# Attention plus gated FFN on one core: head groups in pairs, OUT in two parts, prologue evictions to the idler engine, and a new order of work

## The chip, the core and the metric

The kernel runs on one core of one Trainium2 chip. The metric is the time of one execution in device microseconds (us). A core has several engines that run side by side (in the kernel before, PE, ACT and DVE are busy 90%, 89% and 86% of the same span): PE (matrix multiply, with its own weight loads, PEld), ACT (ScalarE), DVE (VectorE), POOL (GpSimd) and SP (here only a queue that issues DMAs). A run that is over 1.5% above the fastest of its kernel would be called slow. "Clock" is the share of the full PE clock that was granted in the records; it is a mean over a stretch.

## The reference, cut to what matters

```python
xn = layernorm(x)                                   # 2048 rows x 512, no scale, no bias
q, k, v = split_heads(xn @ wqkv)                    # 32 heads of 16
o = softmax(q @ k.T / 4) @ v                        # full attention, 2048 x 2048 per head
out = x + o @ wo + (silu(xn @ w1) * (xn @ w3)) @ w2 # F = 1792
```

The exponentials of attention are most of the work: 32 heads of 2048 x 2048 scores.

## The kernel before: the parts that matter

The rows of queries are cut into 4 chunks of 512 and the heads into 8 groups of 4. One (chunk, group) is a *unit*; there are 32. A unit has 64 score tiles of 128 x 512, which are made and used in *pairs* of two tiles, so there are 1024 pairs in all. A pair's exponentials are taken either by ACT (one instruction) or by DVE (a bit trick in five instructions). PV then multiplies them with V, and an extra column of ones gives the row sums. At the end of a unit a chain copies PV's result to U, moves the sums, inverts them, spreads the inverses over the rows (DMAs to Lc, Rrow, R) and multiplies: the result is a tile of `onorm`.

What is neither scores nor PV is called *dense* work here: Q, K and V tiles, FFN steps (14 per chunk, 8 groups of 4 matmuls each) and OUT tiles (4 per chunk; each sums FFN rows and attention rows into 128 rows of the result).

The order of instructions on each engine is fixed while the kernel is built. A planner in the Python code simulates the engines with modelled durations and emits instructions in the order in which its model would start them. Where a model was wrong, an engine waits in that order: in the changed kernel's trace PE stands 2.06 us before 644 us, for one late multiply, with scores behind it.

```python
# what PE takes next, in this order
elif try_a() or try_d() or try_pv() or try_dense():      # ACT scores, DVE scores, PV, dense

# FFN of a chunk waits for all of OUT of the chunk before
if sc > 0 and not all(("OUT", (sc - 1) * 4 + i) in done for i in range(4)):
    return False

# OUT: 14 groups over FFN rows, then 8 over attention rows (4 heads x 16 rows of 128 used)
for fc in range(FC):
    gr.append((hT[:, fc, ...], w2[:, fc, :], ...))
for g in range(NG):                                      # NG = 8
    gr.append((onorm[:, (qc * NG + g) % NON, ...], wo[:, g, :], ...))

# prologue: one score buffer, no DVE exponentials while "early"
bufs = [0]
if not st["early"] and idle((2, 3)):
    bufs = [0, 1]
# ... (cut)
```

## Time and profile before

| | value | where it is read |
|---|---|---|
| time | 887.0 us, median of 4 runs (883.5 to 888.4) | timed runs |
| busy over the span | PE 90%, ACT 89%, DVE 86% | page, part 1 |
| last exponential on ACT starts at | 825.3 us | instructions of the exp line |
| last FFN eviction starts at | 857.6 us | instructions of its line |

Three lines of the page of the kernel before: the busy time of each engine over the whole span, then for ACT the busy tenths and for PE the granted clock in tenths, in 40 slices of 22.2 us.

```profile
PE 797.7 (90%) x8985; PEld 223.4 (25%) x8985; DVE 766.3 (86%) x999; ACT 791.6 (89%) x885; POOL 59.4 (7%) x59
ACT  2689999999889999999999999999999999999310
PEclk9999999999569999999999999999999999999878
```

The averages alone mislead: three engines near 90% look balanced. The strips show stages. Counted from 1, ACT is full from slice 4 to slice 37 apart from a dent at slices 11 and 12, just where the clock falls to 5 and 6 tenths, and it is all but idle in the last three.

The same by stretches, from the windows view of the kernel before. Columns: stretch and its length, busy us and number of instructions of PE, PEld, DVE, ACT and POOL, then granted clock, DMA share and GB/s.

```profile
54.00:220.00 166.00, 152.59 (x1695) 41.20 (x1693) 154.51 (x196) 164.94 (x187) 7.69 (x6) 0.99 0.27 38
220.00:260.00 40.00, 38.39 (x246) 7.00 (x244) 30.67 (x36) 34.87 (x36) 2.58 (x2) 0.53 0.19 15
260.00:640.00 380.00, 354.59 (x3998) 95.76 (x3996) 350.69 (x440) 376.31 (x419) 23.61 (x15) 1.00 0.25 32
640.00:660.00 20.00, 17.99 (x194) 4.79 (x190) 19.51 (x25) 19.46 (x23) 1.56 (x1) 1.00 0.29 35
660.00:827.00 167.00, 156.56 (x1802) 42.86 (x1804) 156.24 (x200) 165.51 (x184) 9.42 (x7) 1.00 0.26 33
827.00:886.00 59.00, 38.03 (x559) 15.51 (x553) 16.13 (x29) 3.59 (x6) 0.00 (x0) 0.79 0.20 39
```

In the long stretches ACT is busy 99% of the time: the exponentials set the pace, and dense work gets what PE has over. In 220:260 ("the hole") PE is 96% busy and yet runs only 246 matmuls, at a clock of 0.53: FFN of chunk 0 is done, FFN of chunk 1 must wait for OUT, and OUT for the last unit's chain. This is why PE's busy share can't be read as PE's progress: at that clock (0.50 in 222:258) a score matmul shows 0.60 us, at full clock (270:400) 0.39.

In 827:886 ("the tail") ACT has nothing to do. Three lines of the timeline of the kernel before show why; the bracket at the end of a line is the idle time before it and what ended it.

```profile
829.72 1.32 PE L1222 MATMUL ps<-f_xnT,f_w 128*32 128x512 bf16 x12 [2.32 <-DMA f_w<-in_B_w_dram]
835.82 2.74 PE L1222 MATMUL ps<-f_xnT,f_w 128*32 128x512 bf16 x32 [2.83 <-DMA f_w<-in_B_w_dram]
842.20 3.60 PE L1222 MATMUL ps<-f_xnT,f_w 128*32 128x512 bf16 x32 [3.64 <-DMA f_w<-in_B_w_dram]
```

Seven FFN steps are left over after attention, PE waits four times for their weights from HBM (2.3 to 3.6 us each), and all of the last chunk's OUT comes after them.

### The profile page before, as it was taken

To read this page: it belongs to the slowest core of one execution; us is meant where nothing else is said; L and a number is where in the kernel's file an instruction comes from. 1 tells how busy PE (TensorE), PEld (TensorE's weight loads), DVE (VectorE), ACT (ScalarE), POOL (GpSimd) and SP (SyncE) were. 2 spreads that over 40 slices of the span, in tenths; PEclk is the share of its full clock that TensorE was granted. 3 is DMA by queue.
4 is the path that set the end of the run, shared out by engine and by line. 5 is a ranking of instruction groups with operands and counts; after the bars stand their busy time and mean duration, and the time that the engine had idled before them with its cause. 6 is when DMAs were issued, how large, how long until landed. Compare 5 with 4: busy or idle time off the path is not lost.

```text
span 886.3 us, 21031 instructions
## 1 busy us (share of the span) xinstructions
PE 797.7 (90%) x8985; PEld 223.4 (25%) x8985; DVE 766.3 (86%) x999; ACT 791.6 (89%) x885; POOL 59.4 (7%) x59
## 2 busy tenths in 40 slices
PE   4899998998999999999989999989889999989586
PEld 1322222222112222222222222222222222222132
DVE  6879998999778999989989999989999999999332
ACT  2689999999889999999999999999999999999310
POOL 4200001000000000011000000000000000000000
PEclk9999999999569999999999999999999999999878
DMA  8713223123112223221322223231222222333311
GB/s 306 170 31 50 31 38 55 26 37 38 7 14 26 21 27 45 28 43 29 48 32 20 32 26 38 38 37 26 33 30 44 20 26 20 44 44 38 50 26 40
DMA packets 88471, 38.42 MB, mean 43 GB/s; under 512 B 71472, under 2 KB 85552, under 8 KB 88368
## 3 DMA queue, kind: packets, MB, share of 16 engines
q1 hardware_dynamic: 88368, 36.99, 27.4%
q8 instruction: 72, 1.18, 0.6%
q14 instruction: 31, 0.25, 0.1%
HBM read 22.81 MB, written 2.10 MB: 28 GB/s over the span
## 4 chain that ended last, share of the span: by engine, by line
ACT 60%; PE 20%; DVE 15%; DMA 2%; issue 2%; SPq 0%; DVEq 0%
ACT f_PT L1571 57%; PE ps L1222 10%; PE ps L1533 6%; DVE f_xd L1623 5%; PE ps L1736 4%; DVE f_xd L1669 3%; ACT f_th L1350 2%; DVE f_xd L1683 2%; DVE f_xd L1662 1%; DVE f_xd L1678 1%; DMA f_w<-in_B_w_dram 1%; DMA f_wkv<-in_A_wqkv_dram 1%; DVE f_hT L1364 1%; DVE f_t L1354 1%; DVE f_xn_sb L1412 1%
## 5 line engine op out<-in xcount | busy, mean ns | idle before, releaser
L1571 ACT ACTIVATE f_PT<-ps 128x1024 bf16<-128x1024 f32 x810 | 761.3, 1094 | 21.4 <-PE ps L1533 18.1
L1533 PE MATMUL ps<-f_QT,f_KT 32*128 32x512 bf16 x2048 | 330.2, 395 | 38.7 <-ACT f_PT L1571 30.1
L1623 DVE TENSOR_SCALAR f_xd<-ps 128x1024 int16<-128x1024 f32 x214 | 261.2, 1221 | 33.9 <-PE ps L1533 26.4
L1736 PE MATMUL ps<-f_PT,f_Vaug 128*17 128x512 bf16 x1620 | 232.3, 394 | 5.1 <-DVE f_xd L1678 1.6
L1736 PE MATMUL ps<-f_xd,f_Vaug 128*17 128x512 bf16 x1284 | 182.0, 393 | 3.0 <-DVE f_xd L1683 0.9
L1222 PE MATMUL ps<-f_xnT,f_w 128*32 128x512 bf16 x1792 | 157.2, 401 | 18.2 <-DMA f_w<-in_B_w_dram 11.4
L1533 PEld LDWEIGHTS ps<-f_QT,f_KT 32*128 32x128 bf16 x2048 | 82.0, 91 | 355.6 <-ACT f_PT L1571 312.6
L1669 DVE TENSOR_TENSOR f_xd<-f_xd 128x2048 bf16<-128x2048 bf16 (+1 forms) x119 | 132.4, 1112 | 0.0
L1789 POOL TENSOR_TENSOR f_onorm<-f_U,f_R 128x512 bf16<-128x512 f32 x31 | 44.9, 1447 | 733.6 <-DMA f_R<-f_Rrow 529.8
L1662 DVE TENSOR_SCALAR f_xd<-f_xd 128x2048 int16<-128x2048 int16 (+1 forms) x119 | 78.8, 662 | 6.3 <-PE ps L1736 4.1
L1683 DVE TENSOR_SCALAR f_xd<-f_xd 128x2048 int16<-128x2048 int16 (+1 forms) x119 | 82.0, 689 | 2.0
L1678 DVE TENSOR_SCALAR f_xd<-f_xd 128x2048 int16<-128x2048 int16 (+1 forms) x119 | 78.3, 658 | 2.6
L1736 PEld LDWEIGHTS ps<-f_PT,f_Vaug 128*17 128x17 bf16 x1620 | 53.4, 88 | 104.7 <-issue 85.1
L1222 PE MATMUL ps<-f_w,f_hT 128*32 128x512 bf16 x896 | 71.9, 386 | 1.7 <-DVE f_hT L1364 1.3
L1350 ACT ACTIVATE f_th<-ps 128x512 f32<-128x512 f32 x56 | 38.0, 679 | 26.9 <-PE ps L1222 26.9
L1222 PEld LDWEIGHTS ps<-f_xnT,f_w 128*32 128x32 bf16 x1792 | 42.0, 98 | 75.0 <-issue 48.2
L1736 PEld LDWEIGHTS ps<-f_xd,f_Vaug 128*17 128x17 bf16 x1284 | 41.1, 88 | 43.9 <-issue 22.3
L1354 DVE SCALAR_TENSOR_TENSOR f_t<-f_th,ps 128x512 bf16<-128x512 f32 x56 | 38.2, 683 | 13.4 <-ACT f_th L1350 13.1
L1364 DVE SCALAR_TENSOR_TENSOR f_hT<-f_t,ps 128x512 bf16<-128x512 bf16 x56 | 38.2, 682 | 13.1 <-PE ps L1222 12.9
L1222 PE MATMUL ps<-f_wo,f_onorm 128*32 128x512 bf16 x512 | 40.2, 381 | 0.2 <-DVE f_wkv L1404 0.2
L1222 PEld LDWEIGHTS ps<-f_w,f_hT 128*32 128x32 bf16 x896 | 20.8, 96 | 23.0 <-issue 9.5
L1222 PE MATMUL ps<-f_wkv,f_xnT 128*32 128x512 bf16 x256 | 21.3, 434 | 3.5 <-DMA f_wkv<-in_A_wqkv_dram 3.5
(52 smaller groups left out, 220.4 us busy)
## 6 DMA issues: line engine op xcount, KB each, us to landing
f_w<-in_B_w_dram SPq DMA_DIRECT2D x112, 128.0 KB, 3.0
f_R<-f_Rrow SPq DMA_DIRECT2D x128, 32.0 KB, 4.4
f_KT<-f_hT SPq DMA_DIRECT2D x6, 512.0 KB
f_KT<-f_stg SPq DMA_DIRECT2D x32, 64.0 KB, 1.9
f_QT<-f_stg SPq DMA_DIRECT2D x32, 64.0 KB, 3.1
f_xr<-in_A_x_dram SPq DMA_DIRECT2D x16, 128.0 KB, 2.2
out_dram<-f_xn_sb SPq DMA_DIRECT2D x16, 128.0 KB
f_w<-in_B_w_dram SPq DMA_DIRECT2D x1, 1792.0 KB
```

The lines of the kernel that those rows point to most:

```text
L1222: ins = e.matmul(bank(bk)[32 * i:32 * i + 32, 0:ncols], make_lhsT(i), rhs_ap, start=start, stop=stop, tile_position=(0, 32 * i))
L1350: q = P.op("act", lambda e: e.activation(th[:, ss, :], bank(bk), ACTF.Tanh, scale=0.5), reads=[("ps", bk)], writes=[("th", ss)], dur=a_cos ...
L1354: q2 = P.op("dve", lambda e: e.scalar_tensor_tensor(t1[:, ss, :], th[:, ss, :], 1.0, bank(bk), ALU.add, ALU.mult), reads=[("th", ss), ("ps ...
L1364: q = P.op("dve", lambda e: e.scalar_tensor_tensor(hT[:, fc, :], t1[:, ss, :], 0.5, bank(bk), ALU.mult, ALU.mult), reads=[("t1", ss), ("ps ...
L1533: ins = e.matmul(bank(b), l_, r_, start=True, stop=True, tile_position=(rp, 0))
L1571: q = P.op("act", lambda e: e.activation(PT[:, s_, :], ps[:, b0 * 512:(b0 + 2) * 512], ACTF.Exp, scale=ASC, bias=ABIAS), reads=[("ps", b0) ...
L1623: q = P.op("dve", lambda e: e.tensor_scalar(dsl[:, ys, 1024 * c:1024 * c + 1024], ps[:, 4 * 512:6 * 512], 0.0, 32767.0, ALU.max, ALU.min), ...
L1662: P.op("dve", lambda e: e.tensor_scalar(dsl[:, NY + m_, 0:n], y, 0x7F, 0x3F00, ALU.bitwise_and, ALU.bitwise_or), reads=[("ds", ys)], write ...
L1669: q_ = P.op("dve", lambda e: e.tensor_tensor(t_ap.bitcast(BF16), y.bitcast(BF16), t_ap.bitcast(BF16), ALU.mult), reads=[("ds", ys)], write ...
L1678: q_ = P.op("dve", lambda e: e.tensor_scalar(g_ap, y, -352.0, 0.0, ALU.add, ALU.max), reads=[("ds", ys)], writes=[("ds", NY + NM + g_)] + ...
L1683: q_ = P.op("dve", lambda e: e.tensor_scalar(y, y, 0x7F80, None, ALU.bitwise_and), reads=[], writes=[("ds", ys)], dur=s_cost(n), name="e")
L1736: ins = e.matmul(bank(PV)[32 * j:32 * j + 17, :], v_, p_, start=s0, stop=s1, tile_position=(0, 32 * j))
```

## The change

Its intent, part by part:

- **Group pairs** (of head groups; not the pairs of score tiles above). Two head groups share one tile of `onorm` and one of `wo`: the odd unit's result sits in rows 16 to 31 of each 32. OUT has 4 attention groups in place of 8 (64 groups of 4 matmuls fewer in all). PV of odd units has 32 weight columns in place of 17 to land in those rows, and 64 small DMAs move the rows together.
- **Split.** OUT of chunks 0 to 2 becomes an FFN part (added to x, kept in `osum`) and an attention part. FFN of the next chunk waits only for the FFN part.
- **Prologue.** An eviction of V or of a transpose goes to whichever of ACT and DVE is idle first; two score buffers; no FFN before the early tiles are done; DVE exponentials from the last transpose on.
- **Order.** PE takes dense work before PV while fewer than `PVQ` = 8 PV tasks wait.

```diff
-    NON = 11
+    NON = 6
+    NP = NG // 2
+    PVQ = 8
...
-        wo = sb("wo", [128, NG, D], BF16)
+        wo = sb("wo", [128, NP, D], BF16)
...
-                P.post("dve", emit, ready=o.end + _LAT, prio=prio)
+                P.post2({"dve": emit, "act": emit_a}, ready=o.end + _LAT, prios={"dve": prio, "act": 2})
...
-                if sc > 0 and not all(("OUT", (sc - 1) * 4 + i) in done for i in range(4)):
+                if sc > 0 and not all(("HF", (sc - 1) * 4 + i) in done for i in range(4)):
...
-            for g in range(NG):
-                if part == 1 and g == NG - 1 or part == 2 and g < NG - 1:
+            for g in range(NP):
+                if part == 1 and g == NP - 1 or part == 2 and g < NP - 1 or part == 3:
                     continue
...
+            if sc > 0:
+                for ts in range(4):
+                    bg.append(tile_OUT(sc * 4 - 4 + ts, 4))
             for ts in range(4):
-                bg.append(tile_OUT(sc * 4 + ts, 1 if sc == NQC - 1 else 0))
+                bg.append(tile_OUT(sc * 4 + ts, 1 if sc == NQC - 1 else (3 if sc < 3 else 0)))
...
-            if not st["early"] and idle((2, 3)):
+            if idle((2, 3)):
...
+                w_ = Vaug[:, tk[1], 4 * (g // 2) + j, 0:17] if g % 2 == 0 else Vaug[:, tk[1], 4 * (g // 2) + j, 1:33]
...
+                if h:
+                    for j in range(4):
+                        P.dma(lambda e, j=j: e.dma_start(U[32 * j + 16:32 * j + 32, 0, :], U[32 * j + 16:32 * j + 32, 1, :]),
+                              reads=UK, writes=[("Uo", j)], kb=32)
...
-                    elif try_a() or try_d() or try_pv() or try_dense():
+                    elif try_a() or try_d() or (backlog() < PVQ and st["pos"] < NR and try_dense()) or try_pv() or try_dense():
```

More of the change, by code (lines that the diff above doesn't have):

```diff
@@ L174, in post, with post2 @@
         self.pend[eng].append((prio, self.seq, ready, cond, emit))
+    def post2(self, emits, ready=0.0, prios=None, cond=None):
+        self.seq += 1
+        its = {}
+        for e, emit in emits.items():
+            it = ((prios or {}).get(e, 1), self.seq, ready, cond, emit, its)
+            its[e] = it
+            self.pend[e].append(it)
     def pump(self, eng):
@@ L182, in pump @@
             return False
-        self.pend[eng].remove(best)
+        if len(best) > 5:
+            for e, it in best[5].items():
+                self.pend[e].remove(it)
+        else:
+            self.pend[eng].remove(best)
         best[4]()
@@ L1041, in _plan_fast @@
         KT = sb("KT", [128, NG, S], BF16)
-        Vaug = sb("Vaug", [128, NT, H, 17], BF16)
+        Vaug = sb("Vaug", [128, NT, H // 2, 34], BF16)
         QT = sb("QT", [128, 4, 512], BF16)
@@ L1067, in _plan_fast @@
         w2_v = B_w2.rearrange("(c p) n -> p c n", p=128)
-        wo_v = A_wo.rearrange("(g j d) n -> j d g n", j=4, d=16)
+        wo_v = A_wo.rearrange("(g h j d) n -> h j d g n", h=2, j=4, d=16)
         XD = [("x", t) for t in range(NT)]
@@ L1169, in _plan_fast @@
             P.post("dve", lambda gi=gi: stat([4 * gi + 2, 4 * gi + 3]), ready=7.0 + 3 * gi, prio=3)
-        def c_late(e):
-            e.memset(R[:, :], 0.0)
-            return e.memset(wo[:, :, :], 0.0)
-        def late0():
-            o = P.op("pool", c_late, writes=[("wo",)] + [("R", j_) for j_ in range(4)], dur=3.5)
-            done["wo0"] = o.end + _LAT
-        P.post("pool", late0, ready=12.0, prio=2)
         def wv_check():
@@ L1213, in late_loads @@
             for j in range(4):
-                P.dma(lambda e, j=j: e.dma_start(wo[32 * j:32 * j + 16, :, :], wo_v[j]), reads=[("wo",)],
-                      writes=[("wor", j)], kb=128)
+                for h in range(2):
+                    P.dma(lambda e, j=j, h=h: e.dma_start(wo[32 * j + 16 * h:32 * j + 16 * h + 16, :, :], wo_v[h, j]),
+                          writes=[("wor", j, h)], kb=64)
             P.dma(lambda e: e.dma_start(w2[:, :, :], w2_v), writes=[("w2",)], kb=1792)
-        P.post("sp", late_loads, ready=20.0, prio=2, cond=lambda: "wo0" in done)
+        P.post("sp", late_loads, ready=20.0, prio=2)
         def col_groups(make_lhsT, rhs_ap, ncols):
@@ L1233, in emit, with emit_a @@
                     q = P.op("dve", lambda e: e.tensor_copy(dst, src_fn(bk)), reads=[("ps", bk)], writes=[key],
-                             dur=d_cost(n))
+                             dur=d_cost(n), name="evV")
                     done[dkey] = q.end + _LAT
                     rel(q)
-                P.post("dve", emit, ready=o.end + _LAT, prio=prio)
+                def emit_a():
+                    q = P.op("act", lambda e: e.activation(dst, src_fn(bk), ACTF.Identity), reads=[("ps", bk)],
+                             writes=[key], dur=a_cost(n), name="evV")
+                    done[dkey] = q.end + _LAT
+                    rel(q)
+                P.post2({"dve": emit, "act": emit_a}, ready=o.end + _LAT, prios={"dve": prio, "act": 2})
             return evac
@@ L1248, in evac, with emit_a, emit_d @@
                 tb = bank(bk).bitcast(BF16)[:, 0:DC * 128].rearrange("p (c s) -> p c s", s=128)
-                eng = "act" if (t < 4 and t % 2 == 0) or t >= 4 else "dve"
-                def emit():
-                    if eng == "act":
-                        q = P.op("act", lambda e: e.activation(xnT[:, :, t * 128:(t + 1) * 128], tb, ACTF.Identity),
-                                 reads=[("ps", bk)], writes=[("xnT", t)], dur=a_cost(512))
-                    else:
-                        q = P.op("dve", lambda e: e.tensor_copy(xnT[:, :, t * 128:(t + 1) * 128], tb),
-                                 reads=[("ps", bk)], writes=[("xnT", t)], dur=d_cost(512))
+                def emit_a():
+                    q = P.op("act", lambda e: e.activation(xnT[:, :, t * 128:(t + 1) * 128], tb, ACTF.Identity),
+                             reads=[("ps", bk)], writes=[("xnT", t)], dur=a_cost(512), name="evT")
                     done[("xnT", t)] = q.end + _LAT
                     rel(q)
-                P.post(eng, emit, ready=o.end + _LAT, prio=0)
+                def emit_d():
+                    q = P.op("dve", lambda e: e.tensor_copy(xnT[:, :, t * 128:(t + 1) * 128], tb),
+                             reads=[("ps", bk)], writes=[("xnT", t)], dur=d_cost(512), name="evT")
+                    done[("xnT", t)] = q.end + _LAT
+                    rel(q)
+                P.post2({"act": emit_a, "dve": emit_d}, ready=o.end + _LAT, prios={"act": 0 if t < 8 else 2, "dve": 0})
             return _T("TR%d" % t, [(f, [("xn", t % 4), ("ident",)], None, 0.3)], evac,
@@ L1323, in tile_V @@
                 gr.append((lambda e, bk, c=c: col_groups(
-                    lambda i: xnT[:, c, t * 128 + 32 * i:t * 128 + 32 * i + 32], wv[:, c, :], D)(
+                    lambda i: xnT[:, c, t * 128 + 32 * i:t * 128 + 32 * i + 32], wv[:, c, :].rearrange("p (i h x) -> p h i x", h=2, x=64), D)(
                         e, bk, c == 0, c == DC - 1), [("wv",), ("xnT", t)], None, DG))
             return _T("V%d" % t, gr, evac_copy(
-                Vaug[:, t, :, 0:16], lambda bk: bank(bk).rearrange("p (h d) -> p h d", d=16), ("V", t), ("V", t), prio=1),
+                Vaug[:, t, :, :].rearrange("p a (h e) -> p h a e", h=2)[:, :, :, 0:16],
+                lambda bk: bank(bk).rearrange("p (h a d) -> p h a d", h=2, d=16), ("V", t), ("V", t), prio=1),
                 cond=xc)
@@ L1385, in tile_OUT @@
             gr = []
-            if part != 2:
+            if part not in (2, 4):
                 for fc in range(FC):
@@ L1389, in tile_OUT @@
                                [("hT", fc), ("w2",)], None))
-            for g in range(NG):
-                if part == 1 and g == NG - 1 or part == 2 and g < NG - 1:
+            for g in range(NP):
+                if part == 1 and g == NP - 1 or part == 2 and g < NP - 1 or part == 3:
                     continue
-                gr.append((lambda i, g=g: onorm[:, (qc * NG + g) % NON, ts * 128 + 32 * i:ts * 128 + 32 * i + 32], wo[:, g, :],
-                           [("ON", (qc * NG + g) % NON), ("wo",)] + [("wor", j_) for j_ in range(4)],
+                gr.append((lambda i, g=g: onorm[:, (qc * NP + g) % NON, ts * 128 + 32 * i:ts * 128 + 32 * i + 32], wo[:, g, :],
+                           [("ON", (qc * NP + g) % NON)] + [("wor", j_, h_) for j_ in range(4) for h_ in range(2)],
                            lambda g=g: have(("ON", qc, g))))
@@ L1402, in e1 @@
                 def e1():
-                    if part == 1:
+                    if part in (1, 3):
                         q = P.op("dve", lambda e: e.tensor_tensor(osum[:, ts, :], bank(bk), xr[:, ts % 2, :], ALU.add),
@@ L1410, in e1 @@
                         return
-                    other = osum[:, ts, :] if part == 2 else xr[:, ts % 2, :]
+                    other = osum[:, ts, :] if part in (2, 4) else xr[:, ts % 2, :]
                     q = P.op("dve", lambda e: e.tensor_tensor(osb[:, ts, :], bank(bk), other, ALU.add),
-                             reads=[("ps", bk), ("osum", ts) if part == 2 else ("xr", ts % 2)],
+                             reads=[("ps", bk), ("osum", ts) if part in (2, 4) else ("xr", ts % 2)],
                              writes=[("osb", ts), ("xn", ts)],
@@ L1420, in e1 @@
                            ready=q.end + _LAT, prio=1)
-                P.post("dve", e1, ready=o.end + _LAT, prio=1, cond=lambda: part == 2 or ("xr", tg) in done)
+                P.post("dve", e1, ready=o.end + _LAT, prio=1, cond=lambda: part in (2, 4) or ("xr", tg) in done)
             def cond():
-                if part == 2:
-                    return have(("OSUM", tg), ("ON", qc, NG - 1))
+                if part in (2, 4):
+                    return have(("OSUM", tg), ("ON", qc, NP - 1))
                 if not have(*[("hT", qc, fc) for fc in range(FC)]):
                     return False
-                g_need = NG - 2 if part == 1 else NG - 1
+                if part in (1, 3) and qc > 0 and ("OUT", (qc - 1) * 4 + ts) not in done:
+                    return False
+                if part == 3:
+                    return have(*[("KTm", NG - 1, i_) for i_ in range(NQC)])
+                g_need = NP - 2 if part == 1 else NP - 1
                 return have(("ON", qc, g_need))
@@ L1434, in start @@
                 P.post("sp", load, ready=P.t, prio=1, cond=lambda: tg < 2 or ("XE", tg - 2) in done)
-            return _T("O%d_%d" % (tg, part), groups, evac, cond=cond, start=None if part == 2 else start)
+            return _T("O%d_%d" % (tg, part), groups, evac, cond=cond, start=None if part in (2, 4) else start)
         st = {"pos": 0, "pv": 0, "dpar": 0, "nd": 0, "lastA": -1.0, "n_exp": 0, "pm": ("col", None, 0.0)}
@@ L1489, in early_phase @@
         def early_phase():
-            return any(z[0] == 0 for z in crit[:4])
+            return any(z[2].name[:2] == "TR" for z in crit[:16])
         def dense_banks():
@@ L1495, in dense_banks @@
             if st["early"]:
-                return [6, 2, 3, 4, 5]
+                return [6, 4, 5]
             return [6]
@@ L1729, in try_pv @@
                 stop = st["pos"] >= (u + 1) * RPU and npv[u][j] == NT + 2 * ndj[u][j]
-                mms.append((j, Vaug[:, tk[1], 4 * g + j, :], tk[2], start, stop))
+                w_ = Vaug[:, tk[1], 4 * (g // 2) + j, 0:17] if g % 2 == 0 else Vaug[:, tk[1], 4 * (g // 2) + j, 1:33]
+                mms.append((j, w_, tk[2], start, stop))
                 rd += [("V", tk[1]), tk[3]]
@@ L1735, in f @@
                 for (j, v_, p_, s0, s1) in mms:
-                    ins = e.matmul(bank(PV)[32 * j:32 * j + 17, :], v_, p_, start=s0, stop=s1, tile_position=(0, 32 * j))
+                    ins = e.matmul(bank(PV)[32 * j:32 * j + (17 if g % 2 == 0 else 32), :], v_, p_, start=s0, stop=s1, tile_position=(0, 32 * j))
                 return ins
@@ L1748, in unit_end @@
         def unit_end(u, o):
-            us = u % 2
-            qc, g = divmod(u, NG)
+            h = u % 2
+            qc, pi = divmod(u // 2, NP)
+            UK = [("Uc",)] + [("Uo", j_) for j_ in range(4)] if h == 0 else [("Ut",)]
             def e0():
-                q = P.op("dve", lambda e: e.tensor_copy(U[:, us, :], bank(PV)), reads=[("ps", PV)], writes=[("U", us)],
-                         dur=d_cost(512))
+                q = P.op("dve", lambda e: e.tensor_copy(U[:, h, :], bank(PV)), reads=[("ps", PV)], writes=UK,
+                         dur=d_cost(512), name="U")
                 pvb[0] = q.end + _LAT
@@ L1758, in e1 @@
             def e1():
-                q = P.dma(lambda e: e.dma_start(Lc[:, u, :], U[16:128:32, us, :]), reads=[("U", us)],
-                          writes=[("Lc", u)], kb=8)
+                r0 = 16 - h
+                q = P.dma(lambda e: e.dma_start(Lc[:, u, :], U[r0:128:32, h, :]), reads=UK, writes=[("Lc", u)], kb=8)
+                if h:
+                    for j in range(4):
+                        P.dma(lambda e, j=j: e.dma_start(U[32 * j + 16:32 * j + 32, 0, :], U[32 * j + 16:32 * j + 32, 1, :]),
+                              reads=UK, writes=[("Uo", j)], kb=32)
                 P.post("dve", e2, ready=q.end + _LAT, prio=0)
@@ L1776, in e3 @@
                 q = P.dma(lambda e: e.dma_start(Rrow[:, :], Rc[:, :]), reads=[("Rc",)], writes=[("Rrow",)], kb=8)
-                P.post("sp", e4, ready=q.end + _LAT, prio=0, cond=lambda: u == 0 or ("e5", u - 1) in done)
+                P.post("sp", e4, ready=q.end + _LAT, prio=0, cond=lambda: u < 2 or ("e5", u // 2 - 1) in done)
             def e4():
@@ L1781, in e4 @@
                     q = P.dma(lambda e, j=j: e.dma_start(
-                        R[32 * j:32 * j + 16, :], Rrow[j:j + 1, :].unsqueeze(1).broadcast_to([1, 16, 512])),
-                        reads=[("Rrow",)], writes=[("R", j)], kb=32)
-                eng = "dve" if u == NU - 1 else "pool"
-                P.post(eng, lambda: e5(eng), ready=q.end + _LAT, prio=0,
-                       cond=lambda: u < NON or all(("OUT", (u - NON) // NG * 4 + i) in done for i in range(4)))
-            def e5(eng):
-                q = P.op(eng, lambda e: e.tensor_tensor(onorm[:, u % NON, :], U[:, us, :], R[:, :], ALU.mult),
-                         reads=[("U", us)] + [("R", j_) for j_ in range(4)], writes=[("ON", u % NON)],
-                         dur=0.65 if eng == "dve" else 1.3)
-                done[("ON", qc, g)] = q.end + _LAT
-                done[("e5", u)] = q.end
-            P.post("dve", e0, ready=o.end + _LAT, prio=0, cond=lambda: u < 2 or ("e5", u - 2) in done)
+                        R[32 * j + 16 * h:32 * j + 16 * h + 16, :], Rrow[j:j + 1, :].unsqueeze(1).broadcast_to([1, 16, 512])),
+                        reads=[("Rrow",)], writes=[("R", j, h)], kb=32)
+                if h:
+                    eng = "dve" if u == NU - 1 else "pool"
+                    P.post(eng, lambda: e5(eng), ready=q.end + _LAT, prio=0, cond=lambda: u // 2 < NON or all(
+                        ("OUT", (u // 2 - NON) // NP * 4 + i) in done for i in range(4)))
+            def e5(eng):
+                on = (u // 2) % NON
+                q = P.op(eng, lambda e: e.tensor_tensor(onorm[:, on, :], U[:, 0, :], R[:, :], ALU.mult),
+                         reads=[("Uc",)] + [("Uo", j_) for j_ in range(4)] +
+                         [("R", j_, h_) for j_ in range(4) for h_ in range(2)], writes=[("ON", on)],
+                         dur=0.65 if eng == "dve" else 1.45)
+                done[("ON", qc, pi)] = q.end + _LAT
+                done[("e5", u // 2)] = q.end
+            P.post("dve", e0, ready=o.end + _LAT, prio=0, cond=lambda: u < 2 or h == 1 or ("e5", u // 2 - 1) in done)
         def dense_cands(lst):
@@ L1812, in start_tile @@
                 tl = None
-                for x in bg[:3]:
+                cand = bg[:3] + [x for x in bg[3:] if x.name[0] == "O" and x.name.endswith("_4")]
+                if cand and any(z[0] == 0 for z in crit[:4]):
+                    cand = []
+                cand.sort(key=lambda x: not x.name.endswith("_4"))
+                for x in cand:
                     if x.cond is None or x.cond():
@@ L1844, in try_dense @@
                     if a.name[0] == "O":
-                        done[("OUT", int(a.name[1:].split("_")[0]))] = o.end
+                        tg_, pt_ = a.name[1:].split("_")
+                        if pt_ != "3":
+                            done[("OUT", int(tg_))] = o.end
+                        if pt_ in "013":
+                            done[("HF", int(tg_))] = o.end
                     a.evac(bk, o, rel)
@@ L1848, in try_dense, with backlog @@
             return False
+        def backlog():
+            return sum(len(tasks[u][j]) for u in range(pv_unit[0], min(NU, pv_unit[0] + 2)) for j in range(4))
         def fin():
```

## The prediction

> **What bounds the kernel now.** Page, part 1: PE 90%, ACT 89%, DVE 86% of 886.3 us. By stage (windows view):
>
> - Prologue, 0 to 54 us: PE busy 27.2 of 28 us from 26 to 54, yet only some 20 exps ran, single-buffered; ACT busy 19.4 of 28. Two FFN steps ran there.
> - Steady stage, 54 to 826: ACT busy 98 to 100%. The chain of waits is 57% exps. FFN and OUT get what PE has over: about one 4-matmul group per us.
> - A hole, 220 to 262: chunk 0's FFN ends near 219; the next must wait for OUT 0, which waits for unit 7's normalised rows (POOL multiply at 256). No dense work; the granted clock falls to 0.50, exps from 11.7 per 10 us to 11, 10, 10, 8: about 8 lost.
> - Tail, 827 to 886: ACT idle. The timeline shows 7 FFN steps still to do (829 to 858, waiting 2.3 to 3.6 us each for w loads), then OUT (858 to 877), then 9 us from the last adds to the end.
>
> [...]the clock halves when dense work runs out and is 1.00 again by 260:270, as OUT begins.
>
> **Removed.** 256 of OUT's 512 attention matmuls: 64 groups of four. The tail's timeline gives 0.215 us a group: 13.8 us of PE, 10.3 before the tail, 3.4 in it. Half of the 32 POOL multiplies (1.3 us, off the chain).
>
> **Added.** 12 more DVE adds of 0.68 us: 8.2 us. 64 DMAs of 32 KB on the SP queue, about 0.6 us of issue each, four in the last unit's chain. Odd units' PV weights have 32 columns for 17: loads about 96 for 88 ns, hidden.
>
> **Moved.** FFN of chunk n+1 starts after the FFN part of OUT n: the hole should close, and its clock dip with it. Prologue: no FFN, two score buffers, DVE exps from the last transpose on, V evictions shared: about 5 us sooner at full rate. Dense goes before PV while fewer than 8 PV tasks wait, so PV comes in fuller groups.
>
> **Sum (estimates).** Attention now ends at 827. Prologue -5, hole -7 (8 exps of 0.92), DVE adds +2 (8.2 us is 3 pairs, which ACT takes over): 817. Dense groups after the prologue: 844; at 1.02 per us, the rate outside the hole, some 785 are done by then. The 59 left are about the first OUT parts of chunk 3. They fit under the last unit's chain (827.2 to 842.2 today). Then one group per tile, adds and store: 10 us. Tail 25 in place of 59.
>
> Predicted: 843 us; 8 in 10 between 828 and 866. Faster by over 2%: 0.94; within 2%: 0.05; slower: 0.01.
>
> **Right or wrong by:** OUT attention matmuls 256; clock 1.00 through 220:262; exps near 12 per 10 us there; last exp at 815 to 820; FFN's last eviction before or within 5 us of it; no w waits in the tail; ACT idle for 25 us at the end; last-unit chain 15 to 18 us.
>
> **What would make it wrong.** Dense work finishing early, so that the clock halves in the last stage. FFN steps left over after all: 4 us each with their loads. SP's 64 new issues delaying w loads or the last chain. PV starved by the new priority, so exps wait for PT slots.

827 - 5 - 7 + 2 = 817 for the end of attention, and the tail of 25 makes 842; the forecast is 843. Its 96 and 88 ns are mean weight loads of 32 and of 17 columns on the page of the kernel before; that the difference would be hidden was an estimate.

## The result, and the profile after

The changed kernel took 856.0 us (median of 4, 854.0 to 857.6) against 887.0 us: a ratio of 0.9655, 95% interval 0.9619 to 0.9692. Ratios here are the mean time of one kernel's fast runs over that of the kernel before's in the same rounds, so they are not quite the ratios of the medians. The time lies in the predicted range (828 to 866), 13 us above the predicted middle.

The same three lines of the page, now of the changed kernel (slices of 21.3 us):

```profile
PE 764.9 (90%) x8693; PEld 214.3 (25%) x8693; DVE 738.3 (86%) x975; ACT 797.3 (93%) x893; POOL 30.9 (4%) x41
ACT  4589999999999999999999999999996999999990
PEclk9899999999999999999999999999996999999996
```

The dent at 220 us is gone, and of the three near-empty slices at the end one is left. There is a new dent in slice 31, and the clock falls with it.

The windows view of the changed kernel, same stretches (its span ends at 853.8):

```profile
54.00:220.00 166.00, 152.17 (x1734) 42.12 (x1730) 146.58 (x186) 161.99 (x183) 4.43 (x3) 1.00 0.29 43
220.00:260.00 40.00, 38.62 (x470) 10.62 (x466) 34.62 (x42) 39.59 (x44) 1.28 (x1) 1.00 0.27 32
260.00:640.00 380.00, 357.23 (x4086) 98.40 (x4086) 355.55 (x455) 379.04 (x425) 9.47 (x7) 1.00 0.29 38
640.00:660.00 20.00, 17.94 (x148) 3.48 (x140) 10.23 (x13) 13.42 (x15) 1.61 (x1) 0.66 0.11 23
660.00:827.00 167.00, 152.78 (x1706) 42.46 (x1704) 154.85 (x196) 166.43 (x188) 4.66 (x3) 1.00 0.28 35
827.00:886.00 59.00, 11.14 (x159) 4.03 (x157) 7.42 (x16) 4.14 (x5) 0.00 (x0) 0.85 0.11 16
```

In 220:260 PE does 470 matmuls in place of 246 in the same busy time, at clock 1.00. In 640:660 it is the other way round: 148 for 194, clock 0.66, ACT 13.4 us busy in place of 19.5.

Where the time went is best read by counting pairs (exponential instructions on ACT plus first steps on DVE, each counted once, in the stretch in which it starts; a windows view shows up to one more per engine and edge, because it counts what crosses an edge on both sides). "Order back" is a run of the experiments below, in which only `PVQ` is 0.

| stretch, us | before: ACT + DVE | changed | order back (pvq0) |
|---|---|---|---|
| 0 to 80 | 42 + 8 | 45 + 6 | 48 + 9 |
| 80 to 220 | 145 + 37 | 145 + 35 | 146 + 36 |
| 220 to 260 | 35 + 11 | 42 + 11 | 42 + 11 |
| 260 to 640 | 395 + 106 | 396 + 105 | 398 + 104 |
| 640 to 660 | 20 + 6 | 14 + 3 | 21 + 6 |
| last exp starts, us | 825.3 | 830.1 | 814.8 |
| last FFN eviction starts, us | 857.6 | 783.9 | 820.1 |
| span, us | 886.3 | 853.8 | 844.6 |

By 640 us the changed kernel is 6 pairs ahead of the kernel before (1 more in the prologue, 7 in the hole, 2 fewer in between). In 640:660 it loses 9 and is 3 behind. Attention then ends 5 us *later* than before. The whole gain of 32 us is in the tail: from the last exp to the end 61 us before, 24 us now. The prediction had attention end at 817.

Two places in the changed kernel's trace explain most of that. First the timeline around 642 us (lines of the other engines, and of weight loads and PV, left out):

```profile
642.34 1.61 POOL L1820 TENSOR_TENSOR f_onorm<-f_U,f_R 128x512 bf16<-128x512 f32 x1 [47.14 <-DMA f_R<-f_Rrow]
644.00 0.62 PE L1230 MATMUL ps<-f_wo,f_onorm 128*32 128x512 bf16 x4 [2.06 <-POOL f_onorm L1820]
644.54 0.61 PE L1556 MATMUL ps<-f_QT,f_KT 32*128 32x512 bf16 x4
645.19 1.02 ACT L1594 ACTIVATE f_PT<-ps 128x1024 bf16<-128x1024 f32 x1 [2.31 <-PE ps L1556]
```

An attention part of OUT stands in PE's order before the scores that follow it. The planner took the spread of the inverses to land 2.1 us after its issue; the page shows a median of 4.0. So POOL multiplied late, PE waited 2.06 us for it with all scores behind it, and ACT waited too. The longer price comes after: each matmul now shows 0.61 in place of 0.39 us, and the clock reads 0.50 until 657.

Second, the prologue. From the waits view of PE in the changed kernel (what waits, for whom, then total us, count and longest us of the waits):

```profile
PE ps L1556 <- DMA f_KT<-f_stg: 6.0, 1, 6.0
```

One move of K tiles held PE up for 6 us. The timeline of the SP queue, which issues the DMAs, shows what was issued around it:

```profile
28.52 0.63 SPq L1224 DMA_DIRECT2D f_w<-in_B_w_dram  x1
29.26 3.13 SPq L1303 DMA_DIRECT2D f_KT<-f_stg  x2
```

The load at 28.52 is all of w2, 1.8 MB, first used at 229 us. The move of K tiles that scores need next is issued right behind it. It landed 9.7 us later (chain of waits); the median of such moves is 2.0 us. PE stood 6 us and the clock halved from 36 to 43 us. The kernel before has the same load in front of a K move, which took 8.4 us there, but its PE does not stand for it: its list of waits has no such line.

The tail is as predicted. Some 24 dense groups of OUT still run in it: 20 of the last chunk's first parts under the last chain, and the 4 last parts after it. The timeline of the changed kernel, last lines (PEld and SP lines left out):

```profile
844.21 0.69 DVE L1820 TENSOR_TENSOR f_onorm<-f_U,f_R 128x512 bf16<-128x512 f32 x1 [7.22 <-DMA f_R<-f_Rrow]
844.96 1.90 PE L1230 MATMUL ps<-f_wo,f_onorm 128*32 128x512 bf16 x16 [8.72 <-DVE f_onorm L1820]
845.63 2.49 DVE L1428 TENSOR_TENSOR f_xn_sb<-ps,f_wkv 128x512 bf16<-128x512 f32 x4 [0.72 <-PE ps L1230]
```

At the end of the chain PE waits 8.7 us with nothing else to do; no weights are loaded any more.

### The profile page after: what moved, and what is told of

The parts are those of the page before. It is cut to its first block, busy times and chain, and to the rows that moved or that the text cites. A ratio compares the mean times of both kernels' runs of the same rounds, so it can differ in the third digit from the quotient of the medians.

```text
span 853.8 us, 20404 instructions
## 1 busy us (share of the span) xinstructions
PE 764.9 (90%) x8693; PEld 214.3 (25%) x8693; DVE 738.3 (86%) x975; ACT 797.3 (93%) x893; POOL 30.9 (4%) x41
## 4 chain that ended last, share of the span: by engine, by line
ACT 64%; PE 21%; DVE 8%; DMA 5%; issue 1%; SPq 1%; POOL 0%; DVEq 0%; POOLq 0%
ACT f_PT L1594 61%; PE ps L1230 9%; PE ps L1556 7%; PE ps L1760 5%; ACT f_th L1366 3%; DVE f_xd L1646 2%; DMA f_KT<-f_stg 1%; DVE f_xd L1692 1%; DMA f_wkv<-in_A_wqkv_dram 1%; DMA f_R<-f_Rrow 1%; DVE f_xd L1706 1%; DVE f_xd L1685 1%; DVE f_hT L1380 1%; DMA f_QT<-f_stg 1%; DMA f_Rrow<-f_Rc 0%
## 5 line engine op out<-in xcount | busy, mean ns | idle before, releaser
L1594 ACT ACTIVATE f_PT<-ps 128x1024 bf16<-128x1024 f32 x819 | 769.2, 1095 | 19.4 <-PE ps L1556 18.6
L1646 DVE TENSOR_SCALAR f_xd<-ps 128x1024 int16<-128x1024 f32 x205 | 250.3, 1221 | 32.1 <-PE ps L1556 24.2
L1760 PE MATMUL ps<-f_PT,f_Vaug 128*17 128x512 bf16 (+1 forms) x1638 | 223.1, 389 | 1.3 <-DVE f_xd L1701 0.6
L1760 PE MATMUL ps<-f_xd,f_Vaug 128*32 128x512 bf16 (+1 forms) x1230 | 178.9, 388 | 5.7 <-DVE f_xd L1692 2.2
L1230 PE MATMUL ps<-f_xnT,f_w 128*32 128x512 bf16 x1792 | 150.6, 383 | 8.0 <-DVE f_t L1370 5.9
L1701 DVE TENSOR_SCALAR f_xd<-f_xd 128x2048 int16<-128x2048 int16 (+1 forms) x112 | 74.1, 661 | 2.5
L1685 DVE TENSOR_SCALAR f_xd<-f_xd 128x2048 int16<-128x2048 int16 (+1 forms) x112 | 74.3, 663 | 2.1 <-PE ps L1760 0.2
L1706 DVE TENSOR_SCALAR f_xd<-f_xd 128x2048 int16<-128x2048 int16 (+1 forms) x112 | 74.2, 662 | 2.2
L1230 PE MATMUL ps<-f_w,f_hT 128*32 128x512 bf16 x896 | 75.8, 382 | 0.2 <-DVE f_wkv L1420 0.2
L1760 PEld LDWEIGHTS ps<-f_PT,f_Vaug 128*17 128x17 bf16 (+1 forms) x1638 | 54.2, 91 | 83.3 <-issue 69.1
L1760 PEld LDWEIGHTS ps<-f_xd,f_Vaug 128*32 128x32 bf16 (+1 forms) x1230 | 43.2, 92 | 56.1 <-issue 27.4
L1230 PEld LDWEIGHTS ps<-f_xnT,f_w 128*32 128x32 bf16 x1792 | 39.6, 95 | 59.2 <-issue 48.4
L1820 POOL TENSOR_TENSOR f_onorm<-f_U,f_R 128x512 bf16<-128x512 f32 x15 | 21.4, 1429 | 742.5 <-DMA f_R<-f_Rrow 647.9
L1230 PE MATMUL ps<-f_wo,f_onorm 128*32 128x512 bf16 x256 | 24.9, 432 | 12.4 <-DVE f_onorm L1820 8.7
L1230 PEld LDWEIGHTS ps<-f_w,f_hT 128*32 128x32 bf16 x896 | 21.3, 95 | 19.9 <-issue 11.5
L1778 DVE COPY f_U<-ps 128x512 f32<-128x512 f32 x32 | 21.9, 684 | 4.1 <-PE ps L1760 4.0
```

The lines of the kernel that those rows point to most:

```text
L1230: ins = e.matmul(bank(bk)[32 * i:32 * i + 32, 0:ncols], make_lhsT(i), rhs_ap, start=start, stop=stop, tile_position=(0, 32 * i))
L1594: q = P.op("act", lambda e: e.activation(PT[:, s_, :], ps[:, b0 * 512:(b0 + 2) * 512], ACTF.Exp, scale=ASC, bias=ABIAS), reads=[("ps", b0) ...
L1646: q = P.op("dve", lambda e: e.tensor_scalar(dsl[:, ys, 1024 * c:1024 * c + 1024], ps[:, 4 * 512:6 * 512], 0.0, 32767.0, ALU.max, ALU.min), ...
L1685: P.op("dve", lambda e: e.tensor_scalar(dsl[:, NY + m_, 0:n], y, 0x7F, 0x3F00, ALU.bitwise_and, ALU.bitwise_or), reads=[("ds", ys)], write ...
L1701: q_ = P.op("dve", lambda e: e.tensor_scalar(g_ap, y, -352.0, 0.0, ALU.add, ALU.max), reads=[("ds", ys)], writes=[("ds", NY + NM + g_)] + ...
L1706: q_ = P.op("dve", lambda e: e.tensor_scalar(y, y, 0x7F80, None, ALU.bitwise_and), reads=[], writes=[("ds", ys)], dur=s_cost(n), name="e")
```

## The experiments

Twelve runs in three calls; each call shares its runs of the kernel before (888.2, 886.2 and 886.6 us median). The changed kernel itself is compared by ratios. It was run at another time. All runs gave correct results. The theory: the shortfall of 13 us is a load queue (prologue) and a clock that falls when dense work is late or runs out. The rivals: PE or the evictions bind in the prologue; the clock has other causes; the loss is noise of the planned order.

### w2late: the load of w2 later

```diff
-            P.dma(lambda e: e.dma_start(w2[:, :, :], w2_v), writes=[("w2",)], kb=1792)
         P.post("sp", late_loads, ready=20.0, prio=2)
+        P.post("sp", lambda: P.dma(lambda e: e.dma_start(w2[:, :, :], w2_v), writes=[("w2",)], kb=1792),
+               ready=75.0, prio=2)
```

> The changed kernel with the 1.8 MB load of w2 issued at a modelled 75 us in place of 20 us. Theory (the prologue's gain was lost to the load queue: the K move of 29 us landed only at 38.9 us behind w2, PE stood 6 us and its clock halved): the 6 us wait of scores for that K move goes to under 1.5 us, the granted clock stays 1.00 from 30 to 50 us, exps and DVE pairs done by 80 us rise from 52 to 58 or more, total 4 to 7 us below the changed kernel's 856. Rival (the prologue is bound by PE and evictions, the wait only moves): pairs by 80 us within 2 of 52 and the total within 2 us of 856.

Measured: 847.5 us, ratio 0.9531 (0.9488 to 0.9573); the control (run null below) has 0.9618. The stretch 30:50 in the windows view, first of the changed kernel:

```profile
30.00:50.00 20.00, 13.84 (x146) 3.85 (x142) 7.64 (x17) 12.59 (x14) 1.76 (x4) 0.83 0.33 105
```

and of this run:

```profile
30.00:50.00 20.00, 18.47 (x225) 5.84 (x222) 10.49 (x22) 17.66 (x20) 0.88 (x2) 1.00 0.08 21
```

Wait and clock dip are gone; the moves of K and Q tiles whose landing the profile gives take 1.9 to 2.1 us. Pairs by 80 us: 55 + 7 against 45 + 6. The time falls by 8 us against the control and by 8 (medians) to 11 (ratios) against the changed kernel, more than expected, although the dip at 640 is still there (clock 0.71 in 640:660). The rival falls: PE and the evictions did not bind the prologue.

### rlat: the planner told the real landing time

```diff
-                        reads=[("Rrow",)], writes=[("R", j, h)], kb=32)
+                        reads=[("Rrow",)], writes=[("R", j, h)], kb=32 + 600)
```

(`kb` is only the planner's model of the transfer, not its size.)

> The changed kernel with the planner told that the broadcast of the reciprocals lands 5.1 us after its issue in place of 2.1 us (the trace shows 4.0 us median); no instruction is added or taken away. Theory (the dip at 642 us is a planned order that misses the real landing: PE stood 2.1 us for a normalised pair, then ran at half clock for 13 us): no PE wait above 1 us for the pair's multiply, clock 1.00 from 630 to 670 us and elsewhere after 80 us, exps of 640 to 660 back from 15 to 22 or more, total 6 to 9 us below 856. Rival (the clock falls with the amount of matmul work in that stretch, whatever the wait): a dip of 10 us or more remains somewhere after 80 us and the total stays within 3 us of 856.

Measured: 854.7 us, ratio 0.9628 (0.9588 to 0.9668): no gain that can be told from the control. The windows view of this run shows why:

```profile
640.00:660.00 20.00, 17.81 (x204) 5.01 (x200) 17.07 (x23) 19.23 (x23) 1.47 (x1) 1.00 0.22 38
780.00:792.00 12.00, 9.46 (x86) 2.46 (x84) 11.61 (x17) 12.00 (x14) 0.00 (x0) 1.00 0.20 18
792.00:804.00 12.00, 11.46 (x92) 2.37 (x94) 10.09 (x13) 9.42 (x10) 1.61 (x1) 0.58 0.20 18
```

The wait at 642 is gone, the dip there with it, and 22 exps run in 640:660 in place of 15 (window counts). Of the runs below, null, which only reshuffles the order, keeps the wait and a dip with it:

```profile
648.93 0.62 PE L1230 MATMUL ps<-f_wo,f_onorm 128*32 128x512 bf16 x4 [2.06 <-POOL f_onorm L1820]
```

So the late landing did cause that dip. But a new dip stands at 792: the last FFN step ended at 780.7, the last chunk's OUT waits for its third group pair (multiplied at 795.3), and PE has no dense work between. In 780:792 PE is busy 9.46 of 12 us. Both theory and rival held in part: the clock fell at a wait, and it fell in a stretch without dense work. It need not: the changed kernel has a like stretch, and its clock stays full. The windows view of the changed kernel, dense matmuls alone (`--source L1230`; columns PE, PEld, clock, DMA share, GB/s):

```profile
783.00:796.00 13.00, 0.00 (x0) 0.00 (x0) 1.00 0.19 18
```

### both: w2late and rlat together

> Both edits: w2's load late and the longer modelled landing. If the two losses are separate the gains add: 10 to 15 us below 856, about 843 (the predicted time). If they share a cause or later stages take the gain back: less than 8 us.

Measured: 850.9 us (845.6 to 851.6), ratio 0.9566 (0.9516 to 0.9616): 5 us below 856, the case of less than 8. The gains do not add. The dip at 640 is gone, and one of 14 us in 782:798 (clock 0.57) takes its place; of the prologue only w2late's view is shown here (clock 1.00 in 30:50).

### null: the same instructions in a slightly other order

```diff
-    d_cost = lambda n: 0.145 + 0.001045 * n
+    d_cost = lambda n: 0.148 + 0.001045 * n
```

> A control: one modelled duration of a DVE eviction 3 ns longer, so that the planner gives another order of the same instructions. It tells how much a reshuffled order alone moves the time. Expected: within 4 us of 856; if it moves by 6 us or more, single edits worth less than that can't be told from reshuffling, and the dip at 642 us should then move or vanish too.

Measured: 855.1 us, ratio 0.9618 (0.9578 to 0.9658). Reshuffling alone moved the time by about a microsecond by medians (3 us by ratios), although the dips move: 0.83 in 640:660, and one of 7 us at 795. This is one reshuffle only; by it, differences of 7 us are more than the order's own, and those of 3 us are not.

### early1: dense work for the end

On top of both:

```diff
-                g_need = NP - 2 if part == 1 else NP - 1
+                g_need = 0 if part == 1 else NP - 1
```

> w2's load late, the longer modelled landing, and OUT part 1 of the last chunk may start as soon as its FFN rows and the first normalised pair are there, in place of the third pair (its later groups still wait for their own pair). In the run with the first two edits the dense work ran out near 778 us and the clock was half from 782 to 798. Theory (the clock falls whenever no dense groups are to be had for some 10 us): about 16 groups fill that gap, no dip between 700 us and the last exp, total 844 or less, 5 us or more below the run with two edits (851). Rival (the dip near the end comes from something else, such as fewer scores): a dip of 8 us or more remains after 770 and the total is within 3 us of 851.

Measured: 848.1 us, ratio 0.9589 (0.9533 to 0.9646). The windows view of 782:798 in the run with two edits, and then of 778:798 in this run:

```profile
782.00:798.00 16.00, 15.26 (x112) 2.81 (x104) 15.07 (x19) 13.82 (x15) 1.27 (x1) 0.57 0.28 24
```

```profile
778.00:798.00 20.00, 18.72 (x207) 4.63 (x196) 17.45 (x22) 18.28 (x20) 1.36 (x1) 0.91 0.23 22
```

With dense groups to be had, the dip shrinks from 14 us to about 3.4 (791 to 794). That speaks for the theory and against the rival, though a short dip is left where the theory had none. The time is 3 us lower, not the 5 or more expected, and in another call: as a gain it is not resolved.

### nosplit: OUT whole again

The condition on `HF` becomes the old one on `OUT`, chunks 0 to 2 use the whole tile, the attention parts go.

> The changed kernel with OUT of each chunk whole again and the next FFN waiting for it; the pairs, the prologue and the priorities stay. Theory (the split closes the hole, and without it each chunk now has one because FFN is ahead of attention): dense holes of 15 us or more near 225, 430 and 620, each with a half clock of 10 us or more; total 866 to 880. Rival (the pairs and the tail carry the gain, the split is worth little): no hole or one only, total within 4 us of 856.

Measured: 863.5 us (858.2 to 867.0), ratio 0.9765 (0.9704 to 0.9826), mean clock 0.956 to 0.971 in its runs. The windows view of the hole:

```profile
232.00:258.00 26.00, 24.84 (x158) 4.83 (x154) 17.52 (x21) 22.99 (x24) 1.71 (x1) 0.54 0.18 16
```

The hole and its half clock come back near 230, so the split is what closed it, and with everything else in place it is worth about 1.1% (0.9765 against 0.9655), some 7 to 10 us. Holes near 430 and 620 came too, a little shorter than expected: no dense matmul runs for 12.0 us from 439 and for 10.5 us from 635. But the clock did not fall in them, and the total stayed under the 866 to 880 expected. The windows view of this run, dense matmuls alone:

```profile
440.00:450.00 10.00, 0.00 (x0) 0.00 (x0) 1.00 0.13 19
636.00:645.00 9.00, 0.00 (x0) 0.00 (x0) 1.00 0.17 26
```

So running out of dense work is not enough for a dip. Over the fourteen traces (counting as dense every matmul that is neither scores nor PV) nine stretches of 10 us or more before the last exp have no dense matmul; five have a dip, four (two here, one each in the changed kernel and w2late) have none. Of the 38 dips between 60 us and the last exp, 33 begin in, or within 2 us after, a stretch of 3 us or more without dense matmuls, and 4 at PE's wait for a late multiply near 640. But there are 118 such stretches, and most have no dip.

### rep64: the 64 groups put back

```diff
+            nrep = {0: 4, 1: 3, 2: 1, 3: 0, 4: 4}[part]
             for k, (lh, rh, rd, cd) in enumerate(gr):
+                for r_ in range(nrep if k == 0 else 0):
+                    groups.append((lambda e, bk, lh=lh, rh=rh: col_groups(lh, rh, D)(e, bk, True, True), rd, cd, DG))
```

> The changed kernel with the first group of OUT tiles issued again until OUT has as many groups as before (64 more groups of four; the result stays right since each repeat overwrites). It puts the pairs' saving in PE work back and nothing else. Prediction's own cost of 0.215 us a group gives 13.8 us of PE. Theory (PE's spare time in the bound stage takes most of it): FFN's last eviction moves from 787 to 825 or later, but the dense work no longer runs out, so total 856 to 866. Rival (PE is the limit throughout): total 868 or more. Second rival (filling work is free or better, since dips vanish): 855 or less.

Measured: 857.0 us, ratio 0.9670 (0.9611 to 0.9728), the same as the changed kernel within the intervals. FFN's last eviction moves from 784 to 833. So in the changed kernel as it is, what the group pairs save on PE is worth nothing that can be told: it only makes FFN end 46 us before the last exp.

### pvq0: PV before dense work again

```diff
-    PVQ = 8
+    PVQ = 0
```

> The changed kernel with PV before dense work again (backlog limit 0). Theory (the priority only moves dense work earlier and fills PV groups, the stage is bound by ACT): total within 5 us of 856, FFN's last eviction later than 787 by 10 us or more. Rival (dense first is what finishes FFN in time): FFN steps left after the last exp and total 862 or more.

Measured: 848.9 us (846.3 to 850.5), ratio 0.9593 (0.9539 to 0.9647), against 0.9655 for the changed kernel: 0.6%, 5 to 7 us. The two intervals overlap a little, but all four times lie below all four of the changed kernel (854.0 to 857.6) and of null. Neither theory nor rival had this: here the priority costs time. The windows view, to be set beside the changed kernel's:

```profile
640.00:660.00 20.00, 19.30 (x226) 5.22 (x220) 18.79 (x26) 20.00 (x23) 0.00 (x0) 1.00 0.26 28
660.00:827.00 167.00, 155.31 (x1801) 45.02 (x1801) 147.11 (x192) 156.35 (x177) 4.28 (x3) 1.00 0.27 37
```

There is no dip anywhere between 80 us and the last exp, which comes at 814.8. FFN's last eviction is at 820, five us after it: dense work lasts to the end. In the prologue DVE's exponentials begin at 50.4 in place of 60.9 us; the table above has 6 pairs of the difference by 80 us and 10 in 640:660, where PE has no wait for a late multiply in this order. By 660 us this run is 19 pairs ahead of the changed kernel and 16 ahead of the kernel before. The tail is longer than the changed kernel's (30 us from the last exp), because it now has OUT of the last chunk in it.

### pvq0_w2late: order back and w2 late

> PV before dense work (limit 0) and w2's load late, together. Theory (two separate losses: the load queue in the prologue, and the dense-first order that lets dense work run out): pairs by 80 us rise from 59 to 66 or more, no clock below 0.9 between 80 us and the last exp, last exp near 808 (it was 815.8 with limit 0 alone). The tail then holds one or two FFN steps more, so total 840 to 845, the best of all. Rival (what attention gains the tail gives back in full, since PE's work is what it is): 847 to 850.

Measured: 845.2 us (840.6 to 846.6), ratio 0.9521 (0.9472 to 0.9570). It is the fastest kernel, 11 us under the changed one by medians, and within the interval of w2late alone (0.9531): with w2's load late, the order back gains nothing that can be told. Pairs by 80 us: 56 + 9, one short of what was expected. The last exp starts at 812.3, not near 808, and three short dips of 3.4 us remain. Among its own four runs the fastest (840.6 us) has the highest mean clock, 0.998, and the slowest (846.6) the lowest, 0.984.

### pvq0_rep64: the 64 groups put back, order back

> Limit 0 with the 64 extra OUT groups of run rep64. With dense first they cost nothing (857 against 856), since dense work ran out anyway. Theory: with limit 0 dense work never runs out before the last exp, so each group put back lands in the tail at 0.215 us or more: total 858 to 866, FFN steps left over in the tail. Rival (PE has slack in the bound stage here too): within 3 us of 849.

Measured: 868.6 us, ratio 0.9786 (0.9748 to 0.9823), against 0.9593 without the repeats: 1.9%, 17 to 20 us. FFN's last eviction is at 841, and the waits of PE have the old tail again:

```profile
PE ps L1230 <- DMA f_w<-in_B_w_dram: 9.8, 3, 4.1
```

The same 64 groups that cost nothing with dense first cost more than their 13.8 us here: the rest of the FFN falls into the tail and waits for weights there.

### pvq0_nosplit: OUT whole, order back

> Limit 0 with OUT whole again and FFN waiting for it. Theory (a hole near 230 with half clock for 12 us or more, as in run nosplit, and its lost dense time, some 20 groups, then sits in the tail): total 858 to 870. Rival (the split is worth under 4 us once dense work is behind PV): 853 or less.

Measured: 853.9 us, ratio 0.9624 (0.9588 to 0.9660). It lies at the edge of the rival's forecast: 5 us above pvq0 by medians, 0.3% by ratios, inside the intervals. In its profile no long dip stands near 230 (one of 3.4 us at 216); one of 10 us stands at 595. What the split is worth in this order stays open.

### pvq0_oldpro: the prologue of before, order back

The two evictions, the end of the early stage, the banks, the single score buffer and FFN in the prologue are as before.

> Limit 0 with the prologue of the kernel before: single score buffer, evictions fixed to their engines, DVE exps only once the early tiles are done, FFN allowed there. Theory (the new prologue is worth 3 to 6 us): pairs by 80 us fall from 59 to 53, total 851 to 856. Rival (FFN steps done in the old prologue pay it back): within 2 us of 849.

Measured: 852.1 us (849.5 to 855.6), ratio 0.9596 (0.9555 to 0.9638), the same as pvq0's 0.9593. Pairs by 80 us fall to 43 + 8 as expected, but the time doesn't follow. The new prologue's own value stays open: 0 by ratios, 3 us by medians, with w2's load in its way; no run tried the two prologues with that load late.

## Why the prediction was right or wrong, point by point

Right:

- OUT has 256 attention matmuls. The hole is closed: clock 1.00 in 220:260, 42 exps started for 35. Run nosplit shows that the split did it.
- No FFN step and no weight load in the tail; ACT idle for 23 us at the end (predicted 25), the last chain 12.5 us from copy to multiply (predicted 15 to 18, so a little long).
- The direction, and in part what it says of the clock: dips begin where dense work has run out, or where PE waits, but not in every such stretch (run nosplit). "Dense work finishing early, so that the clock halves in the last stage" was on the list of what could go wrong. It happened in rlat and both (10 and 14 us at half clock), not in the changed kernel's own trace: there dense work did run out, from 783 to 796, and the clock stayed full.

Wrong in size, by the prediction's own terms:

- **"Dense goes before PV while fewer than 8 PV tasks wait, so PV comes in fuller groups."** It stood in the text without a number, that is, as free. Run pvq0 shows that it cost the changed kernel 5 to 7 us; with w2's load late the same switch moved nothing that can be told (0.9521 against 0.9531). With it FFN ends at 784 us rather than about with attention.
- **"At 1.02 per us ... some 785 are done by then. The 59 left ..."** The count was not far off: at 817 us some 45 groups are left, all of the last chunk's OUT. What the sum had wrong is that dense work comes evenly: FFN ended 46 us before the last exp, and from 783 to 796 there was none, until the third group pair came. So the 13.8 us of PE that the group pairs save are worth nothing in this order (rep64), and 17 to 20 us with PV first (pvq0_rep64).
- **"Prologue -5."** It gained 1 pair by 80 us, less than 1 us at 1.3 pairs per us. w2's load ahead of the K move took the rest; w2late shows 11 pairs more.
- **"Hole -7"** was right (7 pairs), but a new dip of the same size at 640:660 took it back (9 pairs). rlat and null show its cause, a landing modelled at 2.1 us that takes 4.0.
- **"DVE adds +2."** Nothing of it can be seen: in 260:640, with 9 of the 12 adds, both kernels start 501 pairs.

Put together: attention was to end at 817 and ended near 831; the tail came out 2 us shorter than forecast. With `PVQ` = 0 the last exp comes at 815 and the time is 849, nearer the forecast of 817 and 843, but by another way: FFN still runs after the last exp there.

What stays open: the 3 pairs behind at 660 us make about 2.3 us of the 5 by which attention ends later. For the rest, the changed kernel does 222 pairs in 171 us from there and the kernel before 219 in 166. The evictions of four FFN steps more that ACT and DVE have in that stretch could explain it (each is 0.69 us on ACT and 1.36 on DVE), but no run tested that. What PE's clock follows is not shown either. In rlat it fell to 0.58 in 792:804 after 86 matmuls in the 12 us before; in the changed kernel it kept 1.00 with 84 in 12 us (784:796); in the kernel before it read 0.51 from 222 to 260 us while PE counted as busy 36.9 of the 38 us. Nor was it tried why dense first delays DVE's exponentials in the prologue. And the parts, taken out of the changed kernel one at a time, do not add up to its 31 us: the split 7 to 10, the group pairs 0, the order minus 5 to 7. What a part is worth depends on the others, as the two values of the group pairs show, so a share of the gain can't be put down to each.

## What to carry to other kernels

Filler work can be worth keeping for later: finishing it early leaves a hole, and in five of nine holes of 10 us or more here PE's clock fell to half, and the work that bounds the stage slowed: in the hole of the kernel before, a score matmul showed 0.60 us in place of 0.39, and 35 exps started on ACT where the changed kernel started 42. A saving on an engine counts only where its work lies on the path that ends last; the same 64 groups were worth 0 or 17 to 20 us depending on one priority. And where an order is planned ahead from modelled times, check the model against the median landing times of the profile, and look for what large early load stands in front of a small urgent one (here a move of 64 KB took 9.7 us behind 1.8 MB, with a median of 2.0).
